# Query features of pairs 16 to 31: transposed by a crossbar DMA of two 16-bit planes instead of on TensorE, in a new order of all work

## The chip, the cores and the metric

One core of one Trainium2 chip. The metric is device time in microseconds, the median of the timed runs; lower is better. The kernel before takes 957.84 us, the median of 3 runs (957.36 to 957.84).

## The reference

Linear attention with random features, then a two-layer perceptron on its output. B = H = 8, S = 576, D = 64, m = 128 features; 4608 tokens of 512 columns, 2048 hidden columns; float32.

```python
def phi(x):
    proj = np.einsum('bhsd,md->bhsm', x, omega)
    h = proj - np.sum(x * x, axis=-1, keepdims=True) / 2.0
    h = h - np.max(h, axis=-1, keepdims=True)
    return np.exp(h) / np.sqrt(m)
q_p, k_p = (phi(q_s), phi(k_s))                 # q_s, k_s: q, k scaled by D ** -0.25
kv = np.einsum('bhsm,bhsd->bhmd', k_p, v)
z = np.sum(k_p, axis=2)
num = np.einsum('bhsm,bhmd->bhsd', q_p, kv)
den = np.einsum('bhsm,bhm->bhs', q_p, z)[..., None] + 1e-06
x = (num / den).transpose(0, 2, 1, 3).reshape(B * S, H * D)
h = x @ w_in
out = (h / (1.0 + np.exp(-h))) @ w_out
```

## The kernel before, in words

**Attention.** The 64 heads are worked on as 32 pairs, numbered n; four pairs are the 512 columns of one batch of 576 tokens. The 2 x 576 tokens of a pair are 9 blocks of 128 tokens (the middle one is shared by the two heads). For the keys (k) and the queries (q) of a pair, TensorE projects onto the 128 features (`project`, L460, its products in L477; the shared block in `project_mids`, L495). VectorE takes maxima and makes biases; ScalarE exponentiates into a tile of 128 tokens by 9 x 128 features, `hk` or `hq` (`expo`, L536, four instructions of 128 columns to a group, one for the shared block; for some pairs `expo_all`, L557, 1152 columns in one). GpSimd adds the key features over blocks (`sums`, L565 to L570), ScalarE rounds the sums (`sums_high`, L574), TensorE adds them over partitions with a matrix of ones (`zsum`, L587), VectorE forms the denominators from `hq` and that (`denom`, L619) and their reciprocals, and GpSimd divides the query features by them (`normal`, L630, three blocks in each of three instructions).

The numerator needs the query features with the feature on the partition. `turn` (L632 to L637) transposes the nine blocks on TensorE, three to a PSUM bank, and `en_copy` (L640) has ScalarE copy each bank into the tile `en`. `kv` (L595) multiplies keys by values; the result is copied (`kt_copy`, L600), transposed (L603) and copied again (`kw_copy`, L608); `numer` (L657) multiplies `kw` by `en`. For later pairs one unit, `kv_numer` (L665), issues the kv of pair n+1 and then the numerator of pair n. ScalarE copies the attention's output out of PSUM (`x_high`, L679).

**Perceptron.** Each float32 operand is held as a high and a low part, and a product is three TensorE passes (`thrice`, L831, 512 columns each; "main products" below). Batches 0 to 2 go through both layers plainly; the other batches are taken in pairs of batches, (1, 2) to (7, 8), as "levels", with sums and differences of quarters multiplied in seven products (`deep`, L895, for the first layer, `product`, L929, for the second). A level's operands are made from the columns of its two batches (`operand_high`, L889, on ScalarE), its results copied or passed through silu by ScalarE (`deep_copy`, L916; `deep_silu`, L919) and stored. Exponentials and silu use different tables of ScalarE, so that each change between them is an ACT_TABLE_LOAD. Weights come by DMA as `w`, from DRAM copies made earlier (`w_d`, `ws_d`).

**Order.** Each step is a unit with an engine (`Plan.add`, L147, with a duration that the planner assumes). The order of all units on all engines is one table of numbers, `RANK`: units are issued in the order of their ranks, so that each engine works through its own in that order and waits for whatever its next one needs. `HOMES` gives the PSUM pool of each product. `RINGS` gives the number of buffers for each name of a tile: before, two of `hq` and two of `en`. All DMAs are issued on one queue, SP's.

Of the kernel before, what the change touches and what calls it, by code (L numbers as in the profile page):

```python
# [9 lines left out]
F32R = mybir.dt.float32r  # L10
U32 = mybir.dt.uint32
# [7 lines left out]
P = 128  # L19
B, H, S, D = 8, 8, 576, 64  # L20
M = 128
# [19 lines left out]
NORM_DVE = tuple(range(9, 12))  # L41
SQUARES = {}
# [27 lines left out]
    "in": 4, "v": 2, "sq": 2, "hk": 2, "hq": 2,  # L70
    "mxk": 2, "mxq": 2, "nbk": 2, "nbq": 2, "mxm": 2, "nbm": 2, "t": 1, "es": 1, "kt": 1, "kw": 2,
    "en": 2, "den": 2, "rd": 2, "g0": 4, "g1": 4, "g2": 4, "g3": 4, "ts": 3, "w": 7, "ic": 2, "c": 3,
# [67 lines left out]
class Plan:  # L140
# [215 lines left out]
)  # L356
HOMES = (
    "aachcahchaccahahcacachaccaacahaahchccchhcccaaccahhcccaahccachccccachhaachahaaaahahaahaaaahaaaahahaah"
    "aahaacachccaccaccacccahcacacccaaccacacccachccaccaccaacachccachacccaaaccaachacahcaaahahahaahahcccahaa"
    "hchacahhahhcaahccchcaahhahahhacahaahchhacchccaahchhaahhhchahahhaaaahhaahaahhahhhhhchaahcahacachhaaah"  # L360
    "ahcachccahchaahhchhchaaahhhahchaachchcaacahhahhachaahcahcaahahchcachaachahhhaacchhahchaaahhhaaa"
)
# [3 lines left out]
def attention_mlp(ctx: ExitStack, tc: tile.TileContext, qX, kX, qS, kS, qT, kT, qn, kn, v, om_in, w_in, w_out, out):  # L366
# [50 lines left out]
    T = {}  # L417
# [1129 lines left out]
```

## Time and profile before

| | before |
|---|---|
| timed runs | 957.84 us, the median of 3 (957.36 to 957.84) |
| profiled execution, its span | 954.4 us |
| TensorE (PE) busy | 942.7 us, 5740 instructions |
| VectorE (DVE) busy | 772.1 us |
| ScalarE (ACT) busy | 619.8 us, 1184 instructions |
| GpSimd (POOL) busy | 392.4 us |
| DMA | 237.87 MB in 103219 packets |

The profiled execution is one run under the profiler; its span runs from the first to the last instruction and is the time against which its rows add up. The timed runs carry what lies around a span too. Busy is time in which an engine had an instruction at work; it is an average over the whole kernel, which has a stage with attention and perceptron together (to about 700 us) and one with the perceptron alone.

### The profile page before, as it was taken

To read this page: it belongs to the slowest core of one execution; us is meant where nothing else is said; L and a number is where in the kernel's file an instruction comes from. 1 tells how busy PE (TensorE), PEld (TensorE's weight loads), DVE (VectorE), ACT (ScalarE), POOL (GpSimd) and SP (SyncE) were. 2 spreads that over 40 slices of the span, in tenths; PEclk is the share of its full clock that TensorE was granted. 3 is DMA by queue.
4 is the path that set the end of the run, shared out by engine and by line. 5 is a ranking of instruction groups with operands and counts; after the bars stand their busy time and mean duration, and the time that the engine had idled before them with its cause. 6 is when DMAs were issued, how large, how long until landed. Compare 5 with 4: busy or idle time off the path is not lost.

```text
span 954.4 us, 16604 instructions
## 1 busy us (share of the span) xinstructions
PE 942.7 (99%) x5740; PEld 771.3 (81%) x5740; DVE 772.1 (81%) x1625; ACT 619.8 (65%) x1184; POOL 392.4 (41%) x430
## 2 busy tenths in 40 slices
PE   9999999999999999999999999999999999999998
PEld 8778888887888888777878888788888878888886
DVE  6899998698648988868988998879999774478964
ACT  7899886788787676897648866663547444225542
POOL 4676567786867676667323234222221000000000
PEclk9999999999999999999999999999999999999999
DMA  6379999989999798957758477646855566556662
GB/s 242 105 222 335 342 343 316 335 320 317 314 327 340 270 353 317 315 192 271 276 165 317 148 270 253 201 166 190 268 187 166 197 246 235 195 188 220 197 212 99
DMA packets 103219, 237.87 MB, mean 249 GB/s; under 512 B 13665, under 2 KB 44513, under 8 KB 103137
## 3 DMA queue, kind: packets, MB, share of 16 engines
q1 hardware_dynamic: 103136, 236.82, 73.0%
q8 instruction: 46, 0.75, 0.3%
q14 instruction: 37, 0.30, 0.1%
HBM read 192.74 MB, written 44.04 MB: 248 GB/s over the span
## 4 chain that ended last, share of the span: by engine, by line
PE 87%; DVE 6%; ACT 3%; DMA 2%; issue 1%; DVEq 0%; ACTq 0%; SPq 0%
PE ps_acc L831 58%; PE ps_h L831 11%; PE ps_att L477 2%; PE ps_att L595 2%; PE ps_h L477 1%; PE ps_att L657 1%; PE ps_h L636 1%; DVE prod L619 1%; PE ps_h L657 1%; PE ps_acc L477 1%; DMA in<-kX 1%; PE ps_h L595 1%; PE ps_acc L636 1%; PE ps_att L636 1%; DMA g<-w_in 1%
## 5 line engine op out<-in xcount | busy, mean ns | idle before, releaser
L831 PE MATMUL ps_acc<-ts,w 128*128 128x512 f32 x2544 | 600.7, 392 | 1.0 <-ACT hk L536 0.5
L831 PEld LDWEIGHTS ps_acc<-ts,w 128*128 128x128 f32 x2544 | 472.0, 188 | 99.0 <-ACT hk L536 0.7
L873 ACT CAST ts<-g 128x1024 fp32r<-128x1024 f32 x112 | 118.3, 1060 | 95.5 <-PE ps_acc L831 86.8
L877 DVE TENSOR_TENSOR ts<-g,ts 128x1024 fp32r<-128x1024 f32 x112 | 144.7, 1300 | 42.7 <-ACT ts L873 42.4
L831 PE MATMUL ps_h<-xq,w 128*128 128x512 f32 x576 | 142.2, 394 | 0.4 <-DVE xq L683 0.4
L831 PEld LDWEIGHTS ps_h<-xq,w 128*128 128x128 f32 x576 | 106.0, 188 | 22.1 <-DVE xq L683 0.9
L923 DVE TENSOR_TENSOR g<-ps_acc,g 128x512 f32<-128x512 f32 x144 | 93.5, 683 | 27.1 <-PE ps_acc L831 26.1
L630 POOL TENSOR_TENSOR hq<-hq,rd 128x384 f32<-128x384 f32 x87 | 81.8, 961 | 80.8 <-DVE rd L625 80.4
L565 POOL TENSOR_TENSOR t<-hk 128x256 f32<-128x256 f32 x64 | 54.8, 869 | 73.6 <-ACT hk L536 45.1
L869 DVE TENSOR_TENSOR g<-g,g 128x1024 f32<-128x1024 f32 x64 | 82.7, 1317 | 0.8 <-ACT g L927 0.6
L578 POOL TENSOR_TENSOR es<-t,es 128x256 fp32r<-128x256 f32 x32 | 27.7, 864 | 85.1 <-ACT es L574 74.0
L745 POOL TENSOR_TENSOR w<-g,w 128x512 fp32r<-128x512 f32 x32 | 46.7, 1474 | 30.7 <-ACT w L741 30.6
L889 ACT CAST ts<-xq 128x1024 fp32r<-128x1024 f32 x21 | 22.3, 1063 | 52.0 <-PE ps_acc L831 46.7
L619 DVE CUSTOM_DVE_ANT_0 prod<-hq,ps_att 128x128 f32<-128x128 f32 (+1 forms) x150 | 42.9, 286 | 10.4 <-PE ps_att L587 5.3
L927 ACT ACTIVATE g<-g 128x1024 f32<-128x1024 f32 x36 | 36.5, 1054 | 13.5 <-DVE g L923 13.4
L446 DVE TENSOR_REDUCE sq<-in 128x9 f32<-128x576 f32 x48 | 34.8, 739 | 11.1 <-ACT in L441 11.1
L570 POOL TENSOR_TENSOR t<-t,hk 64x128 f32<-64x128 f32 x64 | 35.9, 560 | 14.5 <-ACT hk L536 10.7
L950 DVE TENSOR_TENSOR c<-ps_acc,c 128x512 f32<-128x512 f32 x48 | 31.5, 682 | 10.4 <-PE ps_acc L831 10.4
L477 PE MATMUL ps_att<-oms,in 64*128 64x128 f32 x320 | 37.0, 279 | 0.2 <-ACT hk L536 0.2
L893 DVE TENSOR_TENSOR ts<-xq,ts 128x1024 fp32r<-128x1024 f32 x21 | 25.7, 1227 | 12.2 <-ACT ts L889 12.2
L477 PEld LDWEIGHTS ps_att<-oms,in 64*128 64x128 f32 x320 | 32.4, 187 | 3.7 <-issue 1.8
L619 DVE CUSTOM_DVE_ANT_0 prod<-hq,ps_acc 128x128 f32<-128x128 f32 (+1 forms) x100 | 28.6, 286 | 8.4 <-PE ps_acc L587 3.3
(212 smaller groups left out, 1548.3 us busy)
## 6 DMA issues: line engine op xcount, KB each, us to landing
w<-w_d SPq DMA_DIRECT2D x168, 512.0 KB, 4.8
w<-ws_d SPq DMA_DIRECT2D x48, 512.0 KB, 4.6
v<-v SPq DMA_DIRECT2D x32, 320.0 KB, 4.8
out<-c SPq DMA_DIRECT2D x17, 512.0 KB, 4.7
in<-kT SPq DMA_DIRECT2D x24, 352.0 KB, 4.6
in<-qT SPq DMA_DIRECT2D x24, 352.0 KB, 6.2
g<-w_in SPq DMA_DIRECT2D x16, 512.0 KB, 6.2
g<-w_out SPq DMA_DIRECT2D x16, 512.0 KB, 5.8
```

The lines of the kernel that those rows point to most:

```text
L477: nc.tensor.matmul(ps[:, cols], T["raw", n, who][r, o : o + P], oms[r], start=True, stop=True)
L565: nc.gpsimd.tensor_tensor(t[:, i], e[:, 5 * i : 5 * i + 2], e[:, 5 * i + 2 : 5 * i + 4], ALU.add)
L570: nc.gpsimd.tensor_tensor(t[r, i - 3, 0], t[r, i - 3, 0], e[r, MID], ALU.add)
L619: nc.vector.tensor_tensor_reduce(out=prod[r], in0=e[r, c], in1=z[r, j * M : (j + 1) * M], scale=1.0, scalar=GUARD, op0=ALU.mult, op1=ALU.a ...
L630: nc.gpsimd.tensor_tensor(e[:, c], e[:, c], rd[:, c].unsqueeze(2).broadcast_to([P, 3, M]), ALU.mult)
L745: nc.gpsimd.tensor_tensor(lo, T["w", i], hi.bitcast(F32), ALU.subtract)
L831: nc.tensor.matmul(ps, w(a), x[:, b], start=first and n == 0, stop=last and n == 2, **more)
L869: nc.vector.tensor_tensor(out, a, b, ALU.subtract)
L873: nc.scalar.copy(g[:, 0], T["g", p, SOURCE[j], u])
L877: nc.vector.tensor_tensor(g[:, 1], T["g", p, SOURCE[j], u], g[:, 0].bitcast(F32), ALU.subtract)
L923: nc.vector.tensor_tensor(to, T["q", p, chain, i], T["g", p, r, i // 2][:, i % 2], ALU.add)
L927: nc.scalar.activation(g, g, AF.Silu)
```

## The change

For pairs 16 to 31 (`CROSS`) the three `turn` units and three `en_copy` units of a pair are not made. In their place come: `planes` on ScalarE, which copies the normalised query features (as 16-bit words, 2304 to a partition) so that the 1152 first halves of the float32 words stand together and then the 1152 second halves; `cross`, a DMA on SP's queue (`dma_start_transpose`) that transposes the 18 blocks of 128 x 128 16-bit elements from one on-chip tile to another; and `words` on ScalarE, which copies the transposed halves back together into float32. The numerator waits for `words`. Query features, planes, transposed planes and the transposed features share one ring of four buffers, `f`, in place of `hq` and `en` (two each). `RANK` and `HOMES` are new throughout: 3678 units where 3726 were. In the new file the lines behind `normal` stand about 16 further down: `planes` L637, the crossbar DMA L641, `words` L646, `numer` L673, `thrice` L847.

```diff
+CROSS = tuple(range(16, 32))
...
 RINGS = {
...
-    "in": 4, "v": 2, "sq": 2, "hk": 2, "hq": 2,
+    "in": 4, "v": 2, "sq": 2, "hk": 2, "f": 4,
...
-    "en": 2, "den": 2, "rd": 2, "g0": 4, "g1": 4, "g2": 4, "g3": 4, "ts": 3, "w": 7, "ic": 2, "c": 3,
+    "den": 2, "rd": 2, "g0": 4, "g1": 4, "g2": 4, "g3": 4, "ts": 3, "w": 7, "ic": 2, "c": 3,
...
 RANK = (
-    0, 1, 11, 18, 2, 12, 16, 19, 17, 21, 20, 3, 14, 27, 39, 28, 29, 45, 22, 24, 23, 36, 33, 49, 6, 25, 26, 50, 51, 52,
...
+    2, 0, 1, 11, 3, 6, 7, 12, 8, 16, 13, 4, 10, 17, 30, 21, 18, 31, 19, 34, 14, 46, 49, 56, 38, 35, 36, 44, 45, 54, 55,
...
+    def flat(x):
+        return x.rearrange("p c m -> p (c m)")
+
+    def planes(n):
+        T["pl", n] = to = flat(new("f", [P, NC, M])).bitcast(U16)
+        halves = flat(T["h", n, "q"]).bitcast(U16)
+        nc.scalar.copy(to.rearrange("p (b n) -> p b n", b=2), halves.rearrange("p (n b) -> p b n", b=2))
+
+    def cross(n):
+        T["tp", n] = to = flat(new("f", [P, NC, M])).bitcast(U16)
+        nc.sync.dma_start_transpose(out=to.rearrange("p (c t) -> p c t", t=P), in_=T.pop(("pl", n)))
+
+    def words(n):
+        T["en", n] = en = flat(new("f", [P, NC, P]))
+        halves = T.pop(("tp", n)).rearrange("p (b n) -> p b n", b=2)
+        nc.scalar.copy(en.bitcast(U16).rearrange("p (n b) -> p b n", b=2), halves)
...
+            if n in CROSS:
+                continue
             add(("turn", n, g), "PE", 0.246, at(n, 9.5 + 0.1 * g, 44.2 + 0.8 * g), lambda ps, n=n, g=g: turn(n, g, ps),
...
+        if n in CROSS:
+            add(("pl", n), "ACT", 2.1, 0, lambda n=n: planes(n), after=[("norm", n, 2)], alloc=[("f", ("pl", n))], free=[("h", n, "q")])
+            add(("xp", n), "SP", 0.5, 0, lambda n=n: cross(n), after=[("pl", n)], alloc=[("f", ("tp", n))], free=[("pl", n)], lat=4.0)
+            add(("rc", n), "ACT", 2.1, 0, lambda n=n: words(n), after=[("xp", n)], alloc=[("f", ("en", n))], free=[("tp", n)])
```

**TensorE around pairs 18 and 19.** Before, from the products ahead of the transpose of pair 18's kv (L603) on to the kv of pair 20, which is issued with the numerator of pair 19 (`ps_h`, `ps_acc` and `ps_att` are PSUM banks, `ident` the identity for transposes, `ts` and `w` the operands of a main product):

```order
L831 MATMUL ps_acc<-ts,w 128x512 x6
L603 MATMUL ps_h<-ident,kt 128x128
L831 MATMUL ps_acc<-ts,w 128x512 x6
L595 MATMUL ps_h<-hk,v 64x128 x10
L657 MATMUL ps_acc<-en,kw 64x512 x2
L657 MATMUL ps_h<-en,kw 64x64 x2
L636 MATMUL ps_h<-ident,hq 128x128 x3
L636 MATMUL ps_att<-ident,hq 128x128 x3
L603 MATMUL ps_att<-ident,kt 128x128
L636 MATMUL ps_h<-ident,hq 128x128 x3
L587 MATMUL ps_h<-es,ones 128x256 x2
L595 MATMUL ps_acc<-hk,v 64x128 x10
```

and after the change, around the transpose of pair 19's kv (L602) and the kv of pair 20 with the numerator of pair 19:

```order
L847 MATMUL ps_acc<-ts,w 128x512 x6
L602 MATMUL ps_acc<-ident,kt 128x128
L586 MATMUL ps_h<-es,ones 128x256 x2
L594 MATMUL ps_att<-hk,v 64x128 x10
L673 MATMUL ps_acc<-f,kw 64x512 x2
L673 MATMUL ps_att<-f,kw 64x64 x2
L847 MATMUL ps_acc<-ts,w 128x512 x6
L494 MATMUL ps_h<-oms,in 128x128 x2
L847 MATMUL ps_acc<-ts,w 128x512 x36
```

The L636 rows, three transposes each, are gone between the kv and numerator products (L595 and L657 before, L594 and L673 now), and the next 36 passes of main products follow the kv and numerator that are shown, with only a pair of shared-block projections ahead of them.

**ScalarE in that place after the change**, from pair 18's planes copy (its first row) on; the copy at L646 is pair 18's words copy:

```order
L637 COPY f<-f 128x2304
L932 COPY g_5122<-ps_acc 128x512 x2
L535 ACTIVATE hk<-ps_att,nbk 128x128 x4
L935 ACT_TABLE_LOAD
L935 ACTIVATE g_5001<-ps_acc 128x512
L935 ACTIVATE g_5146<-ps_acc 128x512
L607 COPY kw<-ps_att 128x128
L935 ACTIVATE g_5146<-ps_acc 128x512
L646 COPY f<-f 128x2x1152
L535 ACT_TABLE_LOAD
L535 ACTIVATE hk<-ps_h,nbk 128x128 x4
```

and right behind it, from pair 19's planes copy to its words copy and the copy of its transposed kv (the last row), for which the numerator with the main products behind it waits:

```order
L637 COPY f<-f 128x2304
L695 COPY xr<-ps_acc 128x64
L905 CAST ts<-xq 128x1024
L535 ACTIVATE f<-ps_acc,nbm 128x128
L535 ACTIVATE hk<-ps_acc,nbm 128x128
L440 ACTIVATE in<-in 128x576
L599 COPY kt<-ps_acc 128x128
L535 ACTIVATE f<-ps_h,nbq 128x128 x4
L573 CAST es<-t 128x256
L535 ACTIVATE f<-ps_acc,nbq 128x128 x4
L646 COPY f<-f 128x2x1152
L607 COPY kw<-ps_acc 128x128
```

Where before the three copies of a pair (L640) stood close to its numerator, now a copy of 2304 16-bit elements stands before other work of ScalarE and another behind it, with a change of table between them for pair 18.

## Rows read from the trace of the kernel before

**Rows 1.** The page: span, and busy time, share and instructions of each engine.

```profile
span 954.4 us, 16604 instructions
...
PE 942.7 (99%) x5740; PEld 771.3 (81%) x5740; DVE 772.1 (81%) x1625; ACT 619.8 (65%) x1184; POOL 392.4 (41%) x430
```

**Rows 2.** Windows of 100 us: PE, PEld, DVE, ACT, POOL busy (count); clock, DMA share, GB/s.

```profile
400.00:500.00 100.00, 98.43 (x678) 78.11 (x674) 82.76 (x239) 70.30 (x173) 51.59 (x63) 1.00 0.66 229
500.00:600.00 100.00, 100.00 (x606) 81.84 (x606) 91.46 (x182) 74.11 (x147) 33.67 (x33) 1.00 0.71 249
600.00:700.00 100.00, 100.00 (x641) 81.50 (x638) 86.30 (x213) 52.03 (x94) 26.73 (x38) 1.00 0.60 194
```

**Rows 3.** Windows of 20 us, same columns.

```profile
400.00:420.00 20.00, 20.00 (x132) 16.14 (x128) 13.83 (x55) 17.80 (x39) 14.89 (x19) 1.00 0.46 153
420.00:440.00 20.00, 18.52 (x150) 14.10 (x149) 14.02 (x42) 19.35 (x52) 12.27 (x16) 1.00 0.75 258
```

**Rows 4.** TensorE's timeline, 425 to 445 us: start, length, operation [idle before].

```profile
425.43 0.37 PE L477 MATMUL ps_att<-oms,in 64*128 64x128 f32 x1
...
426.52 3.02 PE L831 MATMUL ps_acc<-ts,w 128*128 128x512 f32 x12
429.38 0.49 PE L636 MATMUL ps_acc<-ident,hq 128*128 128x128 f32 x3
429.71 0.49 PE L636 MATMUL ps_h<-ident,hq 128*128 128x128 f32 x3
430.04 0.61 PE L495 MATMUL ps_acc<-oms,in 128*128 128x128 f32 x4
...
432.69 0.50 PE L587 MATMUL ps_att<-es,ones 128*128 128x256 f32 x2 [0.95 <-ACT hk L536]
433.72 1.69 PE L831 MATMUL ps_acc<-ts,w 128*128 128x512 f32 x6 [0.53 <-ACT hk L536]
...
436.84 1.31 PE L595 MATMUL ps_h<-hk,v 128*64 128x128 f32 x20
...
439.06 0.55 PE L636 MATMUL ps_h<-ident,hq 128*128 128x128 f32 x3
```

**Rows 5.** The chain of waits, its longest piece: start, length, engine, tile, line.

```profile
771.68 156.62 PE ps_acc L831 x690
```

**Rows 6.** Groups of TensorE's instructions by shape, line 636: count, busy, mean ns, idle.

```profile
L636 PE MATMUL ps_h<-ident,hq 128*128 128x128 f32 x105 | 17.1, 277 | 0.2
```

**Rows 7.** ScalarE's timeline, 395 to 444 us.

```profile
427.05 0.60 ACT L919 ACTIVATE g<-ps_acc 128x512 f32<-128x512 f32 x1
427.54 1.04 ACT L889 CAST ts<-xq 128x1024 fp32r<-128x1024 f32 x1
428.48 0.60 ACT L919 ACTIVATE g<-ps_acc 128x512 f32<-128x512 f32 x1
...
430.20 1.28 ACT L536 ACT_TABLE_LOAD   x1
431.49 1.14 ACT L536 ACTIVATE hk<-ps_att,nbk 128x128 f32<-128x128 f32 x4
432.51 1.16 ACT L536 ACTIVATE hk<-ps_acc,nbk 128x128 f32<-128x128 f32 x4
433.51 0.42 ACT L536 ACTIVATE hk<-ps_acc,nbm 128x128 f32<-128x128 f32 x1
433.76 0.33 ACT L600 COPY kt<-ps_h 128x128 f32<-128x128 f32 x1
...
435.00 0.80 ACT L441 ACTIVATE in<-in 128x576 f32<-128x576 f32 x1
435.58 0.37 ACT L608 COPY kw<-ps_h 128x128 f32<-128x128 f32 x1
...
439.64 0.48 ACT L640 COPY en<-ps_h 128x384 f32<-128x384 f32 x1
440.02 0.49 ACT L640 COPY en<-ps_att 128x384 f32<-128x384 f32 x1
```

**Rows 8.** Groups of ScalarE's instructions by shape, line 557.

```profile
L557 ACT ACTIVATE hk<-hk 128x1152 f32<-128x1152 f32 x13 | 15.2, 1166 | 2.4 <-DVE hk L546 2.0 <-DVE hk L544 0.3
```

**Rows 9.** Groups of GpSimd's instructions by shape, lines 565, 570, 795.

```profile
L565 POOL TENSOR_TENSOR t<-hk 128x256 f32<-128x256 f32 x64 | 54.8, 869 | 73.6 <-ACT hk L536 45.1 <-ACT hk L557 27.9 <-ACT kt L600 0.4
L570 POOL TENSOR_TENSOR t<-t,hk 64x128 f32<-64x128 f32 x64 | 35.9, 560 | 14.5 <-ACT hk L536 10.7
...
L795 POOL TENSOR_TENSOR ic<-ic 128x256 f32<-128x256 f32 x32 | 28.0, 875 | 2.4
```

**Rows 10.** DMA issues, 380 to 440 us: count, KB each, median us to landing.

```profile
w<-w_d SPq DMA_DIRECT2D x5, 512.0 KB, 6.7
w<-ws_d SPq DMA_DIRECT2D x5, 512.0 KB, 8.2
...
in<-kT SPq DMA_DIRECT2D x4, 352.0 KB, 4.2
```

**Rows 11.** DMA over the whole span: packets and bytes; one kind of issue.

```profile
DMA packets 103219, 237.87 MB, mean 249 GB/s; under 512 B 13665, under 2 KB 44513, under 8 KB 103137
...
out<-c SPq DMA_DIRECT2D x2, 256.0 KB, 2.0
```

More of the change, by code (lines that the diff above doesn't have):

```diff
@@ L10 @@
 F32R = mybir.dt.float32r
+U16 = mybir.dt.uint16
 U32 = mybir.dt.uint32
@@ L168 @@
 RANK = (
[187 rows of a table removed]
[184 rows of a table added]
 )
 HOMES = (
[L358 to L361, printed above, removed]
+    "achaahaccchachcaccahccchaahahccchaccachchahcchcacacchcahccchacccahccccacahaaaaaahaahhaaaaahaahaaahah"
+    "hahahccacahcacccahacaaahcahchcccaacccccaachcaccccacaachccachcahcccacaccchchcahacaahahhaahahahchcahhc"
+    "achahhahacahcacahhacahhahahhahacahahcchachcchcahahahchahcahhahahchaaahchahahcahahhcahchcaachchaacchc"
+    "aahcachccahahaahahahaaahahhhaaacahhaahhcchhahhh"
 )
@@ L479, in project @@
         if n in FOLD or who == "k":
-            T["h", n, who] = new(f"h{who}", [P, NC, M])
+            T["h", n, who] = new("hk" if who == "k" else "f", [P, NC, M])
         if n not in FOLD:
@@ L497, in project_mids @@
         T["pm", n] = ps
-        T["h", n, "q"] = new("hq", [P, NC, M])
+        T["h", n, "q"] = new("f", [P, NC, M])
         T["mxm", n] = new("mxm", [P, 2])
@@ L630, in normal @@
         nc.gpsimd.tensor_tensor(e[:, c], e[:, c], rd[:, c].unsqueeze(2).broadcast_to([P, 3, M]), ALU.mult)
+    def flat(x):
[11 more added lines that the diff above has]
+        nc.scalar.copy(en.bitcast(U16).rearrange("p (n b) -> p b n", b=2), halves)
     def turn(n, g, ps):
         if g == 0:
-            T["en", n] = new("en", [P, NC * P])
+            T["en", n] = flat(new("f", [P, NC, P]))
         for i in range(3):
@@ L1020, in attention_mlp @@
                     order=([("proj", n - 1, "k" if n - 1 in BOTH else who)] if n else []) + ([("mids", n)] if i and not fold else []),
-                    alloc=([(f"h{who}", ("h",) + w)] if fold or not i else []) + ([] if fold else [(f"mx{who}", ("mx",) + w)])
+                    alloc=([("f" if i else "hk", ("h",) + w)] if fold or not i else []) + ([] if fold else [(f"mx{who}", ("mx",) + w)])
                     + [(f"nb{who}", ("nb",) + w)], free=[])
@@ L1037, in attention_mlp @@
                 after=[("raw", n, "k"), ("raw", n, "q"), "omega2"], order=[("proj", n, "k")],
-                alloc=[("hq", ("h", n, "q")), ("mxm", ("mxm", n)), ("nbm", ("nbm", n))], free=[])
+                alloc=[("f", ("h", n, "q")), ("mxm", ("mxm", n)), ("nbm", ("nbm", n))], free=[])
             add(("topm", n), "DVE", 0.34, at(n, 3.5, 6.2 + 5.8), lambda n=n: top_mids(n), after=[("mids", n)])
@@ L1111, in attention_mlp @@
                     after=[("den", n, 2)], order=[("norm", n, g - 1)] if g else [], free=[("rd", n)], port=True)
+            if n in CROSS:
+                continue
             add(("turn", n, g), "PE", 0.246, at(n, 9.5 + 0.1 * g, 44.2 + 0.8 * g), lambda ps, n=n, g=g: turn(n, g, ps),
                 after=[("norm", n, 0 if one else g)], order=[("turn", n, g - 1)] if g else ([("turn", n - 1, 2)] if n else []),
-                alloc=[] if g else [("en", ("en", n))], banks=1, free=[("h", n, "q")])
+                alloc=[] if g else [("f", ("en", n))], banks=1, free=[("h", n, "q")])
             add(("en", n, g), "ACT", 0.37, at(n, 9.6 + 0.1 * g, 44.4 + 0.8 * g), lambda n=n, g=g: en_copy(n, g),
                 after=[("turn", n, g)], free=[bk(("turn", n, g))])
+        if n in CROSS:
+            add(("pl", n), "ACT", 2.1, 0, lambda n=n: planes(n), after=[("norm", n, 2)], alloc=[("f", ("pl", n))], free=[("h", n, "q")])
+            add(("xp", n), "SP", 0.5, 0, lambda n=n: cross(n), after=[("pl", n)], alloc=[("f", ("tp", n))], free=[("pl", n)], lat=4.0)
+            add(("rc", n), "ACT", 2.1, 0, lambda n=n: words(n), after=[("xp", n)], alloc=[("f", ("en", n))], free=[("tp", n)])
         t, k = divmod(n, NPAIR)
@@ L1120, in attention_mlp @@
         x_new = [("xq", ("x", t, k))] if t < ONCE else [] if k % 2 else [("xq", ("xb", t, k // 2))]
-        after = [("kw", n)] + [("en", n, g) for g in range(3)]
+        after = [("kw", n)] + ([("rc", n)] if n in CROSS else [("en", n, g) for g in range(3)])
         free = [("en", n), ("kw", n)]
```

369 rows, old and new, of the table RANK are left out of this document.

## The prediction

> **What bounds the kernel now.** Read the engines' busy shares first: TensorE works in 942.7 of 954.4 us [rows 1], and in the stage the change touches ScalarE has room: 70 of 100 us busy from 400 on, 52 from 600 on, beside 98.4 and 100 on TensorE [rows 2]. So time that TensorE no longer needs is worth its full length, as long as no other engine becomes late. Then ask where another engine is nearly late. In the forty microseconds from 400 to 440, where pairs 17 to 20 come close together because level 1 of the MLP waits for their columns, ScalarE is busy for 17.80 and 19.35 of 20 us, and in the second stretch TensorE falls to 18.52 [rows 3]. The timeline shows why: TensorE stands still 0.95 and 0.53 us until exponentials have run on ScalarE [rows 4]. There ScalarE is the bound already. The change gives work to it.
>
> The profiled execution spans 954.4 us [rows 1]; the median of the timed runs is 957.84, 3.4 more. I work out a difference on the profiled execution and put it on the median.
>
> **TensorE gives up 144 transposes.** Sixteen pairs with nine each. Six in a row start at 429.38, 429.71 and the next operation at 430.04: 0.66 us, 0.11 each [rows 4]; the mean of 277 ns in a group [rows 6] is latency that overlaps. 144 x 0.11 = 15.8 us. Returning to another kind of product costs 0.1 (twelve main products take 2.86 us from 426.52 to 429.38 [rows 4], where the longest unbroken piece of the chain has 690 in 156.62, 0.227 each [rows 5], so 2.72), but most transposes stand beside other small products whose switch stays: 0.7 us in all. **-16.5 us.** All of it is on the path, since TensorE is the bound outside the stretch above. The 1.5 us of standing still in that stretch belong to the old order and go: **-1.5 us.**
>
> **ScalarE gives up 48 copies and gets 32.** A copy of three transposes takes 0.38 us from start to start (439.64 to 440.02 [rows 7]): 48 x 0.38 = 18 us. A planes or words copy has 2304 elements per partition. The nearest row has 1152 in 1.17 us and 0.1 of that overlaps with the next [rows 8]: 2 x 1.07 = 2.1 us. No row has 16-bit operands or a stride of two; the price could be half (1.05, if two narrow elements go in one step) or double. I take 2.1, the nearest row's rate. 32 x 2.1 = 67 us, a net 49 us more. Over the 360 us from 400 on, of which ScalarE has a quarter to a half free [rows 2], this is hidden, except where none is free.
>
> **The stretch of pairs 17 to 19.** I count, in the new order, ScalarE's instructions from the silu that follows level 1's third product of its second operand to the copy of pair 19's kv that pair 19's last product waits for (its end is shown ahead of this). Eight groups of four exponentials at 1.02 (431.49, 432.51, 433.51): 8.2; four single ones at 0.25: 1.0; five table loads at 1.29: 6.5; ten silus and copies of 512 columns at 0.49: 4.9; one cast of 1024: 0.94; two squares at 0.58: 1.2; eight small copies of 0.1 to 0.3, 1.5 in all [rows 7]. That is 24.2, and five planes and words copies make 10.5: 34.7 us, in one queue that cannot be reordered. TensorE's work between the same two points: 54 main products at 0.227, four projections at 1.09 (425.43 to 426.52), two of kv with numerator at 2.22 (436.84 to 439.06), and 2 us of small ones [rows 4, 5]: 23.1 us. The first point needs a product to have finished and the last holds a product up, so TensorE stands still for the difference, **+11.6 us**. What no longer fits is not work in sum but work in this place.
>
> In the same queue stands a wait. The copy of the sums for pair 20 comes 1.8 us of ScalarE's work after the exponentials it depends on; between them GpSimd has five additions at 0.87 and 0.56 [rows 9], 3.7 us, and two of another kind at 0.87 among them. Not waited: 1.9; all waited: 3.6. I take **+2.5 us**.
>
> **The crossbar DMA.** 576 KB from on-chip memory to on-chip memory, 16 of them. No row shows one. Copies of 256 KB land after 2.0 us at best [rows 11]; in 380 to 440, beside the other loads, 352 KB after 4.2 and 512 KB after 6.7 or 8.2 [rows 10]. I take 6.5, just under the shorter of the two rows of the nearest size in this place; ends 2.0 and 8.2. Between a planes copy and its words copy ScalarE has about 5 us of other work for pairs 16 to 18 (for pair 18, in the order shown: two copies, four exponentials, a table load, three silus, a small copy: 4.9). So each of these three is 1.5 us late: **+4.5 us**; pair 19 has 4.6 and the wait above, and is on time. On SP the weight loads, inputs and the v of later pairs queue behind each of these DMAs while it waits for its planes; they are issued some 9 us of products ahead of use, and four to six buffers cover that. I cost them at nothing; if a crossbar DMA holds the queue for its whole landing they lose 4 us of this, and start to be late.
>
> **Pair 23.** The words copy stands behind a copy of a level 1 result (0.5 us), which needs the product just ahead of pair 23's last one; only four projections (0.36 us) lie between on TensorE. 0.5 + 2.1 - 0.4 = **+2.2 us**. The other pairs have 14 to 62 us of TensorE's work between their denominators and their last product and lie within half a microsecond of fitting; I give them nothing at 6.5.
>
> The crossbar's 16 x 0.59 = 9.4 MB beside 237.9 [rows 11] are hidden. Sum: -16.5 - 1.5 + 11.6 + 2.5 + 4.5 + 2.2 = +2.8 us, so **960.6 us**. (0.2%, 1.9 us, is about what a measurement of this kernel can tell.)
>
> **Rivals.**
>
> *Cheap halves.* ScalarE moves 16-bit elements at half price, or DMAs land within the 5 us of cover. With 1.05 per copy the stretch has 29.4 us against 23.1, +6.3 for +11.6, and pair 23 +1.1; with early landings the +4.5 goes. For it: 5 us is well inside the rows; against: nothing here shows a faster copy. The first makes the sum -3.6, the second -1.7, both -8: 954, 956 or 950 us. It decides once the four positive terms make less than 18 us.
>
> *A slow crossbar.* If it lands after 12 us (half more than the longest row), pairs 16 to 19 pay 7 each, 28 for 4.5, and the pairs behind them, with tight fits, a few more: 984 to 995. In its favour: elements of two bytes, and a queue that is busy at 0.75 in this stretch [rows 3]. At 8.2 it is 966, and with planes copies of 4.2 us the stretch alone has 10 more, 971.
>
> *Block by block.* If each of the 18 blocks of 128 by 128 is handled on its own at 1 us (half of the best landing), one takes 18 us and each pair loses 13 beyond its cover; 16 x 13, less some 40 of slack in the roomy pairs: +170, about 1,130. The Trainium skill (VectorE: DVE Perf Modes, The three transpose paths) gives 1309 ns for one such block by DMA and 390 by TensorE. Its TensorE figure is not what this trace shows (0.11 us from start to start), so its DMA figure need not be a rate either; were it one, an estimate from it is 23.6 us per pair and +260 in all.
>
> **How the numbers follow.** The sum with its bounds (957 to 968): 0.50. Cheap halves or early landing: 0.30. Crossbar slow, 968 to 1,000: 0.16. Block by block: 0.04. The range of 8 in 10 reaches from 946 to 985. Faster by over 0.2%: the second case and a little of the first, 0.32. Within 0.2%: 0.19. Slower: 0.49.
>
> **What would show it.** TensorE should have no L636 row for late pairs, and a standstill of 10 us and more between 400 and 440, ended by ScalarE: by words copies ahead of the products of pairs 18 and 19, and by exponentials. ScalarE should be at 20 of 20 there. Planes copies near 2.2 us, crossbar landings 5 to 8. If ScalarE has gaps that end on the crossbar's landing in most pairs, the slow crossbar holds. If TensorE is full from 400 to 440, the count of the stretch is wrong, and the kernel is faster by the 16 us of transposes.

## The result and the profile after

The changed kernel takes 969.8 us (median of 4 runs, 968.99 to 975.07) where the kernel before takes 957.84: ratio 1.0144, 95% interval 1.0117 to 1.0171. The forecast was 960.6 in a range of 946 to 985, on the slower side. The profiled execution spans 968.7 us, 14.3 more than before.

The page's busy times first (they answer [rows 1]). TensorE has 144 instructions and 1.5 us of busy time less, yet its idle time has grown from 11.7 to 27.5 us:

```profile
span 968.7 us, 16331 instructions
...
PE 941.2 (97%) x5596; PEld 759.3 (78%) x5596; DVE 757.5 (78%) x1625; ACT 672.8 (69%) x1168; POOL 385.7 (40%) x430
```

The windows of the changed kernel, in the columns of [rows 2, 3]. ScalarE is busy for 19 to 20 of every 20 us from 400 to 460, TensorE falls to 16.81 and 14.84, and the granted clock falls too, to a mean of 0.83 from 440 to 460 (the third column from the right). The first line is the kernel before in that same window, which is not among the rows ahead (19.91, and a clock of 1.00):

```profile
440.00:460.00 20.00, 19.91 (x135) 15.54 (x134) 18.02 (x44) 12.88 (x37) 15.33 (x17) 1.00 0.90 319
...
400.00:500.00 100.00, 90.61 (x574) 69.86 (x573) 75.02 (x206) 85.70 (x165) 47.86 (x61) 0.97 0.82 257
500.00:600.00 100.00, 98.99 (x600) 78.23 (x599) 94.34 (x201) 82.72 (x146) 28.18 (x31) 1.00 0.73 244
600.00:700.00 100.00, 96.08 (x567) 77.05 (x567) 79.78 (x181) 62.70 (x86) 30.48 (x38) 0.98 0.81 247
...
400.00:420.00 20.00, 19.16 (x126) 15.05 (x125) 15.70 (x51) 19.19 (x37) 13.73 (x17) 1.00 0.70 213
420.00:440.00 20.00, 16.81 (x120) 12.97 (x120) 10.99 (x46) 19.90 (x42) 8.62 (x12) 1.00 0.86 276
440.00:460.00 20.00, 14.84 (x111) 10.56 (x107) 12.42 (x37) 19.06 (x36) 10.31 (x14) 0.83 0.59 181
```

ScalarE's timeline of the changed kernel (against [rows 7]): a planes copy is an L637 row, a words copy an L646 row. From 413.8 to 455 there is no idle time ahead of any row; the first is at 456.33, behind the copy of pair 19's kv (454.80) that TensorE waits for.

```profile
418.13 0.65 ACT L935 ACTIVATE g<-ps_acc 128x512 f32<-128x512 f32 x1
418.80 1.28 ACT L535 ACT_TABLE_LOAD   x1
...
421.57 2.86 ACT L646 COPY f<-f 128x2304 uint16<-128x2304 uint16 x1
...
433.25 2.21 ACT L637 COPY f<-f 128x2304 uint16<-128x2304 uint16 x1
...
440.40 2.81 ACT L646 COPY f<-f 128x2304 uint16<-128x2304 uint16 x1
443.23 1.28 ACT L535 ACT_TABLE_LOAD   x1
444.52 1.14 ACT L535 ACTIVATE hk<-ps_h,nbk 128x128 f32<-128x128 f32 x4
445.54 2.13 ACT L637 COPY f<-f 128x2304 uint16<-128x2304 uint16 x1
...
452.15 2.88 ACT L646 COPY f<-f 128x2304 uint16<-128x2304 uint16 x1
454.80 0.36 ACT L607 COPY kw<-ps_acc 128x128 f32<-128x128 f32 x1
454.95 0.70 ACT L695 COPY xq<-ps_att 128x512 f32<-128x512 f32 x1
456.33 0.58 ACT L695 COPY xq<-ps_acc 128x512 f32<-128x512 f32 x1 [0.69 <-PE ps_acc L673]
```

TensorE's timeline beside it (against [rows 4]), four of the rows that waited, with the length of the wait and what ended it in brackets: a words copy, exponentials, and the kv copy.

```profile
443.26 1.08 PE L673 MATMUL ps_att<-f,kw 128*64 128x512 f32 x4 [1.34 <-ACT f L646]
...
445.72 0.58 PE L476 MATMUL ps_h<-oms,in 64*128 64x128 f32 x1 [1.26 <-ACT hk L535]
...
449.30 3.23 PE L847 MATMUL ps_acc<-ts,w 128*128 128x512 f32 x6 [1.51 <-ACT hk L535]
...
455.21 1.08 PE L673 MATMUL ps_acc<-f,kw 128*64 128x512 f32 x4 [1.05 <-ACT kw L607]
```

The new copies in the groups by shape (count, busy us, mean ns, idle before), which had no row before:

```profile
L646 ACT COPY f<-f 128x2304 uint16<-128x2304 uint16 x16 | 45.2, 2824 | 4.5 <-DMA f<-f 4.4
L637 ACT COPY f<-f 128x2304 uint16<-128x2304 uint16 x16 | 34.2, 2137 | 3.7 <-POOL f L629 2.9 <-DMA f<-f 0.8
```

And the new DMA in the view of DMA issues, with its count and the median us to landing:

```profile
f<-f SPq DMA_TRANSPOSE x16, 3.9
```

A second place stands out, at pair 25: SP is held 5.71 us by the issue of that pair's crossbar DMA (some 2 us for most others), the DMA lands 9.2 us after the start of its issue, ScalarE waits 2.70 us for it and TensorE 2.93 for ScalarE. It is no accident of one execution: in each of the seven further traces with a crossbar DMA for pair 25, it lands after 7.4 to 8.6 us. The three fences are the timelines of SP, ScalarE and TensorE:

```profile
602.63 5.71 SPq L641 DMA_TRANSPOSE f<-f  x1
608.39 1.05 SPq L843 DMA_DIRECT2D w<-w_d  x2
```

```profile
611.95 2.75 ACT L646 COPY f<-f 128x2304 uint16<-128x2304 uint16 x1 [2.70 <-DMA f<-f]
```

```profile
614.75 1.08 PE L673 MATMUL ps_acc<-f,kw 128*64 128x512 f32 x4 [2.93 <-ACT f L646]
```

To put these side by side I priced every one of TensorE's steps (a projection, six main products, a kv with numerator, ...) at the median time, in the trace of before, from its start to the start of the next, for the same kind of step with the same kind behind it. The sum is TensorE's work; what a step took beyond its price is time lost, by standing or at the lower clock. In us, by the changed kernel's times (the columns from "plain DMA" on are experiments below, in their order plain_dma, whole_words_plain, no_copies_plain, splice, late):

| | before | changed | plain DMA | half copies | no copies | splice | late |
|---|---|---|---|---|---|---|---|
| work | 933.5 | 917.4 | 917.4 | 917.4 | 917.4 | 917.9 | 922.4 |
| lost, 0 to 346 | 7.8 | 13.6 | 14.3 | 18.2 | 14.7 | 7.3 | 7.7 |
| 346 to 404 | 0.8 | 1.4 | 1.6 | 1.6 | 1.1 | 0.9 | 0.7 |
| pairs 17 to 21, 404 to 474 | 3.0 | 15.4 | 15.2 | 9.3 | 9.1 | 15.8 | 3.5 |
| 474 to 607 | 1.6 | 5.3 | 5.4 | 4.3 | 4.6 | 5.8 | 5.8 |
| pairs 25 and 26, 607 to 633 | 0.5 | 5.9 | 1.7 | 1.2 | 1.2 | 5.2 | 3.2 |
| 633 to the end | 2.4 | 4.7 | 4.6 | 4.0 | 4.3 | 4.8 | 4.6 |

From before to the changed kernel: -16.1 of work and +30.2 lost, +14.1 in all, beside 14.3 between the spans (about 5 us of each span lie ahead of the first step and behind the last, outside the rows). (The 18.2 under "half copies" hold a wait of 2.6 us for VectorE and 6.83 us at the lower clock in the first 25 us of that one execution.)

### The profile page after: what moved, and what is told of

Its sections match the earlier page's. It is cut to its first block, busy times and chain, and to the rows that moved or that the text cites. A ratio compares the mean times of both kernels' runs of the same rounds, so it can differ in the third digit from the quotient of the medians.

```text
span 968.7 us, 16331 instructions
## 1 busy us (share of the span) xinstructions
PE 941.2 (97%) x5596; PEld 759.3 (78%) x5596; DVE 757.5 (78%) x1625; ACT 672.8 (69%) x1168; POOL 385.7 (40%) x430
## 4 chain that ended last, share of the span: by engine, by line
PE 67%; DVE 14%; ACT 14%; DMA 2%; issue 2%; POOL 1%; DVEq 0%; SPq 0%; ACTq 0%; POOLq 0%
PE ps_acc L847 48%; PE ps_h L847 8%; ACT f L646 2%; DVE g L939 2%; DVE prod L618 2%; PE ps_att L476 2%; ACT f L535 1%; ACT hk L535 1%; PE ps_att L594 1%; ACT L535 1%; DMA f<-f 1%; PE ps_acc L476 1%; PE ps_att L673 1%; DVE mxq L507 1%; DVE ts L909 1%
## 5 line engine op out<-in xcount | busy, mean ns | idle before, releaser
L847 PE MATMUL ps_acc<-ts,w 128*128 128x512 f32 x2544 | 605.5, 394 | 5.2 <-ACT hk L535 1.5
L847 PEld LDWEIGHTS ps_acc<-ts,w 128*128 128x128 f32 x2544 | 472.1, 188 | 110.4 <-DVE g L939 4.4
L847 PE MATMUL ps_h<-xq,w 128*128 128x512 f32 x576 | 142.9, 396 | 0.9 <-ACT f L656 0.4
L847 PEld LDWEIGHTS ps_h<-xq,w 128*128 128x128 f32 x576 | 105.5, 188 | 23.5 <-DVE xq L699 0.6
L629 POOL TENSOR_TENSOR f<-f,rd 128x384 f32<-128x384 f32 x87 | 84.5, 992 | 87.4 <-DVE rd L624 69.0
L564 POOL TENSOR_TENSOR t<-hk 128x256 f32<-128x256 f32 x64 | 51.4, 817 | 100.8 <-ACT hk L535 47.9
L577 POOL TENSOR_TENSOR es<-t,es 128x256 fp32r<-128x256 f32 x32 | 25.4, 793 | 65.6 <-ACT es L573 64.8
L646 ACT COPY f<-f 128x2304 uint16<-128x2304 uint16 x16 | 45.2, 2824 | 4.5 <-DMA f<-f 4.4
L618 DVE CUSTOM_DVE_ANT_0 prod<-f,ps_acc 128x128 f32<-128x128 f32 (+1 forms) x120 | 34.3, 286 | 10.6 <-PE ps_acc L586 5.3
L618 DVE CUSTOM_DVE_ANT_0 prod<-f,ps_h 128x128 f32<-128x128 f32 (+1 forms) x120 | 34.3, 286 | 8.1 <-PE ps_h L586 2.6
L637 ACT COPY f<-f 128x2304 uint16<-128x2304 uint16 x16 | 34.2, 2137 | 3.7 <-POOL f L629 2.9
L569 POOL TENSOR_TENSOR t<-t,hk 64x128 f32<-64x128 f32 x64 | 32.2, 503 | 9.9 <-ACT hk L535 6.1
```

Of the source, the lines that this page charges most:

```text
L564: nc.gpsimd.tensor_tensor(t[:, i], e[:, 5 * i : 5 * i + 2], e[:, 5 * i + 2 : 5 * i + 4], ALU.add)
L618: nc.vector.tensor_tensor_reduce(out=prod[r], in0=e[r, c], in1=z[r, j * M : (j + 1) * M], scale=1.0, scalar=GUARD, op0=ALU.mult, op1=ALU.a ...
L629: nc.gpsimd.tensor_tensor(e[:, c], e[:, c], rd[:, c].unsqueeze(2).broadcast_to([P, 3, M]), ALU.mult)
L646: nc.scalar.copy(en.bitcast(U16).rearrange("p (n b) -> p b n", b=2), halves)
L847: nc.tensor.matmul(ps, w(a), x[:, b], start=first and n == 0, stop=last and n == 2, **more)
```

## The experiments

**The crossbar DMA replaced by a plain one.**

```diff
-        nc.sync.dma_start_transpose(out=to.rearrange("p (c t) -> p c t", t=P), in_=T.pop(("pl", n)))
+        nc.sync.dma_start(to, T.pop(("pl", n)))
```

> The crossbar DMA is replaced by a plain DMA of the same 576 KB from the same tile to the same tile, so the query features of pairs 16 to 31 are not transposed and the output is not the reference's. Theory 1: from 400 to 460 us ScalarE is busy all the time and waits for no DMA, so the standstill there stays within 1 us of what it was; only the waits for landings around pair 25 (2.7 us of ScalarE's idle time, 2.9 of TensorE's) can go; 965 to 970 us. Theory 2 (the crossbar is what is slow): 960 us or less.

966.9 us, ratio 1.0105 (1.0089 to 1.0120). The windows of the stretch are as in the changed kernel, ScalarE full and TensorE at 16.80:

```profile
420.00:440.00 20.00, 16.80 (x114) 12.94 (x113) 11.40 (x50) 19.90 (x39) 7.64 (x11) 1.00 0.82 285
440.00:460.00 20.00, 14.10 (x116) 10.31 (x115) 12.13 (x37) 19.25 (x35) 11.30 (x15) 0.91 0.49 174
```

The loss at pairs 25 and 26 goes (5.9 to 1.7). There the plain DMA lands after 6.5 us, the crossbar after 9.2. So the crossbar, as a slower DMA, costs some 3 us of the 12 (the intervals of the two ratios touch; it is the trace that shows the place), all of it there; in the stretch of pairs 17 to 21 it costs nothing. The first theory holds.

**Half the elements.** On top of the plain DMA, both copies move float32 words.

```diff
-        nc.scalar.copy(to.rearrange("p (b n) -> p b n", b=2), halves.rearrange("p (n b) -> p b n", b=2))
+        nc.scalar.copy(to, flat(T["h", n, "q"]))
...
-        nc.scalar.copy(en.bitcast(U16).rearrange("p (n b) -> p b n", b=2), halves)
+        nc.scalar.copy(en, T.pop(("tp", n)))
```

> As plain_dma, and in addition the planes and words copies copy 1152 float32 words instead of 2304 16-bit halves: the same bytes, half the elements; the features are neither split nor transposed and the output is not the reference's. To be held against plain_dma (966.9). ScalarE's price: 1.1 to 1.2 us per copy if it goes by elements, 2.1 and 2.8 if by bytes. Theory 1 (ScalarE's queue): with 1.1 to 1.2, the five copies of the stretch are 7 us shorter and TensorE's standstill from 400 to 460 falls by 6 to 7 us: 958 to 961 us. Theory 2 (ScalarE's queue is not what holds TensorE): 965 to 967 us whatever the copies cost.

959.4 us, ratio 1.0025 (1.0010 to 1.0040), 7.5 less than plain_dma. The same bytes in half the elements take 1.17 to 1.18 us for 2.14 and 2.82, so the price goes by elements and not by bytes. (The strides of two went with the halves. In the words copies they may have a share; the planes copy's 0.93 ns an element beside 1.02 here shows none.) The groups by shape:

```profile
L636 ACT COPY f<-f 128x1152 f32<-128x1152 f32 x16 | 18.9, 1180 | 7.4 <-POOL f L629 6.5 <-DMA f<-f 0.9
L644 ACT COPY f<-f 128x1152 f32<-128x1152 f32 x16 | 18.7, 1168 | 1.5 <-DMA f<-f 1.4
```

Two planes copies 0.96 shorter and three words copies 1.65 shorter are 6.9 us; the loss in the stretch falls from 15.2 to 9.3, by 5.9. The theory of ScalarE's queue holds as far as this step goes: almost every microsecond taken out of that queue is one that TensorE gets.

**No copies at all.**

```diff
-        T["pl", n] = to = flat(new("f", [P, NC, M])).bitcast(U16)
-        halves = flat(T["h", n, "q"]).bitcast(U16)
-        nc.scalar.copy(to.rearrange("p (b n) -> p b n", b=2), halves.rearrange("p (n b) -> p b n", b=2))
+        T["pl", n] = flat(T["h", n, "q"])
...
-        T["en", n] = en = flat(new("f", [P, NC, P]))
-        halves = T.pop(("tp", n)).rearrange("p (b n) -> p b n", b=2)
-        nc.scalar.copy(en.bitcast(U16).rearrange("p (n b) -> p b n", b=2), halves)
+        T["en", n] = T.pop(("tp", n))
```

> As plain_dma, without any planes or words copy: the plain DMA goes from the divided query features straight to the tile that the numerator reads. The features are not transposed and the output is not the reference's. Theory 1 (ScalarE's queue): against plain_dma (966.9 us, TensorE standing 15 us between pair 17's sums and pair 22's projection) the 12.7 us of the five copies go and the standstill there falls to 3 to 5 us, and another 2 us elsewhere; 952 to 957 us. What is then left above the kernel before's standstill, less 16 us of transposes, is the new order's own. Theory 2 (the order of that stretch is slow by itself): the standstill stays above 9 us, where halving the copies had left it, and 958 us or more.

958.8 us, ratio 1.0020 (1.0010 to 1.0029): a miss for the first theory; it is the second's 958 us or more, with more than 9 us lost in the stretch. The copies that the run before had left cost 1.2 us each, and taking these away gave TensorE nothing more (9.3 to 9.1 lost in the stretch). The windows show that ScalarE is no longer the limit, 11.10 of 20, and what is in its place: 3 us of standing and the clock at 0.83.

```profile
420.00:440.00 20.00, 19.53 (x161) 15.24 (x161) 14.28 (x50) 18.21 (x46) 10.77 (x14) 1.00 0.92 319
440.00:460.00 20.00, 17.11 (x93) 12.65 (x90) 16.36 (x40) 11.10 (x31) 11.79 (x15) 0.83 0.51 178
```

TensorE's timeline names the waits (exponentials, the low part of a level's operand on VectorE, and the sums of pair 20), and then the lower clock: the twenty products of a kv took 1.31 us in [rows 4], and take 2.40 here.

```profile
441.56 0.50 PE L843 MATMUL ps_acc<-ts,w 128*128 128x512 f32 x1 [0.73 <-ACT hk L535]
443.46 2.01 PE L843 MATMUL ps_acc<-ts,w 128*128 128x512 f32 x5 [1.41 <-DVE ts L905]
...
446.22 0.58 PE L586 MATMUL ps_h<-es,ones 128*128 128x256 f32 x1 [0.53 <-ACT es L573]
...
447.53 2.40 PE L594 MATMUL ps_att<-hk,v 128*64 128x128 f32 x20
```

So ScalarE's copies are 6 of the 12.4 us that the changed kernel loses more in this stretch. Behind them lies a second limit, 6 us more than before. Of the 9.1 us lost here 3.45 is standing (400 to 460: 0.09, 0.47 and 2.89, where the kernel before stood 1.57), and 6.83 us at the lower of the two levels are worth up to 3.4. None of the waits ends on the DMA. ScalarE itself now waits for VectorE, longest 5.3 us for a level's operand and 3.1 for a bias of the exponentials. That this is the new order of the stretch is argued, not shown: no run takes the new order and the clock apart.

**The words copy in another order of elements.**

```diff
-        halves = T.pop(("tp", n)).rearrange("p (b n) -> p b n", b=2)
-        nc.scalar.copy(en.bitcast(U16).rearrange("p (n b) -> p b n", b=2), halves)
+        halves = T.pop(("tp", n)).rearrange("p (b n) -> p n b", b=2)
+        nc.scalar.copy(en.bitcast(U16).rearrange("p (n b) -> p n b", b=2), halves)
```

> The words copy goes through its elements in the order of the output (the two halves of a word one after the other, written side by side, read 1152 elements apart) instead of first all first halves and then all second halves. If the 0.68 us by which a words copy (2.82) is longer than a planes copy (2.14) comes from the stride of two on the written side, it falls to 2.1 to 2.2; by theory 1 the three words copies of the stretch then give TensorE 2 us back: 966.5 to 968.5 us. If it comes from anything else, 2.8 and 969 to 970 us.

967.8 us, ratio 1.0116 (1.0095 to 1.0137). The copy falls to 2.41, between the two expectations:

```profile
L646 ACT COPY f<-f 128x2304 uint16<-128x2304 uint16 x16 | 38.5, 2407 | 3.8 <-DMA f<-f 3.8
```

Going through the elements in the order of the output is worth 0.41 of the 0.68 us. How much the stride of two on the written side costs by itself stays open, since the reading changed with it (from side by side to 1152 elements apart). Three copies 0.41 shorter are 1.2 us, and the loss in the stretch falls by about 1; the time lies where the first theory had it.

**The copies on VectorE.**

```diff
-        nc.scalar.copy(to.rearrange("p (b n) -> p b n", b=2), halves.rearrange("p (n b) -> p b n", b=2))
+        nc.vector.tensor_copy(to.rearrange("p (b n) -> p b n", b=2), halves.rearrange("p (n b) -> p b n", b=2))
...
-        nc.scalar.copy(en.bitcast(U16).rearrange("p (n b) -> p b n", b=2), halves)
+        nc.vector.tensor_copy(en.bitcast(U16).rearrange("p (n b) -> p b n", b=2), halves)
```

> All planes and words copies run on VectorE instead of ScalarE, nothing else moves. VectorE has 4 to 9 of 20 us free in each window from 400 to 460. Theory 1 (ScalarE's queue): if such a copy takes 2.4 us or less on VectorE, the standstill from 400 to 460 falls to 2 to 4 us and the time to 957 to 961 us; if it takes over 4 us VectorE becomes the late engine and little is won. Theory 2 (the crossbar's landing holds the products): no change, 968 to 971 us.

1007.2 us, ratio 1.0525 (1.0485 to 1.0564): a miss, though the copies are cheaper there than the expectation asked:

```profile
L646 DVE COPY f<-f 128x2304 uint16<-128x2304 uint16 x16 | 26.0, 1624 | 1.6 <-DMA f<-f 1.5
L637 DVE COPY f<-f 128x2304 uint16<-128x2304 uint16 x16 | 24.7, 1541 | 3.1 <-POOL f L629 3.1
```

The places in the queue had been chosen for ScalarE. VectorE was already busy for 94 of 100 us from 500 to 600 in the changed kernel. Over the whole span TensorE now waits longest for VectorE's words copies (14.4 us in the view of waits). From 400 to 460 ScalarE is no longer full (14.27, 16.03 and 10.98 of 20), and yet TensorE stands 10.4 us there, where it stood 9.2 in the changed kernel: ScalarE's exponentials now wait for their biases, which VectorE makes (10.0 us of such waits). The load has moved to another queue that has no room either, and the run decides nothing between the two theories.

**The new order with TensorE's transposes.** Two kernels put the nine transposes and three copies of a pair where its planes copy stood, for all sixteen pairs and for pairs 16 to 19.

```diff
-CROSS = tuple(range(16, 32))
+CROSS = ()
...
```

(for the second kernel pairs 20 to 31; RANK and HOMES, cut here, are changed to match)

> The new order kept, but all sixteen pairs are transposed by TensorE and copied by ScalarE again, each pair's nine transposes and three copies standing where its planes copy stood. Theory 1 (the new order has ScalarE at its limit from 414 to 455 us only because of the planes and words copies): TensorE has 16 us more work, but the 11 us of standstill between 400 and 460 and the 6 us around 610 to 640 go; what is left is the 6 us that the new order loses in its first 300 us, where nothing was crossed. 965 to 971 us. Theory 2 (the new order as a whole is slower, whoever transposes): the standstill from 400 to 460 stays and the time is 980 us or more. Theory 3 (the order costs nothing, all of the loss is the crossbar and its copies): 957 to 960 us.

> Only pairs 16 to 19 go back to TensorE's transposes, in the place where their planes copies stood; pairs 20 to 31 stay on the crossbar. Theory 1 (ScalarE's queue in that stretch): 36 transposes add 4.1 us to TensorE; the standstill from 400 to 460 us falls from 13 us to about 3; 962 to 965 us, and ScalarE has idle time in the stretch. Theory 2 (the order of that stretch is slow by itself): no less than 969 us, with TensorE still held by exponentials there.

1000.9 and 976.0 us, ratios 1.0466 (1.0446 to 1.0486) and 1.0206 (1.0180 to 1.0232). By their numbers both fall to the second theory (980 or more, no less than 969). But they do not test the order alone. In the place that I gave the transposes one bank serves one group of three after the other, so that a group waits for ScalarE's copy of the one before (13.2 us of such waits in the first kernel, 5.2 in the second), as in this row of the second kernel:

```profile
453.30 0.66 PE L653 MATMUL ps_att<-ident,f 128*128 128x128 f32 x3 [2.23 <-ACT f L657]
```

A further kernel has the transposes of pairs 16, 18 and 19 where their words copies stood, and in different banks.

> Pairs 16 to 19 on TensorE's transposes once more, but the transposes of pairs 16, 18 and 19 stand where the words copies stood (in the first try TensorE reached them before GpSimd's divisions, and transposed through one bank after the other). Theory 1 (ScalarE's queue): 4.1 us more of TensorE's work, 13 us less ScalarE copies in the stretch; standstill from 400 to 460 us down from 13 us to 3 to 6; 963 to 968 us. Theory 2 (the order of that stretch is slow without the copies too): 972 us or more, with ScalarE idle for over 5 of 20 us in the stretch.

969.1 us, ratio 1.0121 (1.0092 to 1.0151; 964.9 to 970.9). The loss in the stretch is 12.1 us, with ScalarE at 13.34 of 20 from 440 to 460 and the clock at 0.83. The time is between the two theories and decides nothing alone. With the run without copies it shows two ways of emptying ScalarE's queue in this order that both lose far more in the stretch than the 3.0 us of the old one.

**The old order up to pair 16.** RANK and HOMES are put together from the old order up to the first maximum of pair 16 and the new one for the rest; at that point four units are done in the one that are not yet done in the other.

> The order of the kernel before up to the first maximum of pair 16 (some 370 us), then the new order for all that is left; the change itself (crossbar, copies, shared ring of four) stays. Theory 1 (the first 300 us lose 6 us to the new order alone): 963 to 965 us, the windows from 100 to 300 us back at TensorE's 99 of 100. Theory 2 (the shared ring, or anything but the order, holds those pairs up): 968 to 970 us.

964.3 us, ratio 1.0076 (1.0058 to 1.0095), as the first theory had it. TensorE's windows in the first stage are those of before again. The first three lines are the splice (the first of them reads 95.15 before and 94.86 in the changed kernel), the next two the kernel before, the last two the changed kernel:

```profile
0.00:100.00 100.00, 95.26 (x810) 80.57 (x811) 85.38 (x243) 88.27 (x198) 62.97 (x77) 1.00 0.71 231
100.00:200.00 100.00, 100.00 (x603) 82.31 (x602) 85.43 (x182) 77.56 (x142) 71.92 (x74) 1.00 0.98 340
200.00:300.00 100.00, 98.97 (x658) 80.30 (x657) 73.22 (x197) 82.39 (x166) 73.35 (x79) 1.00 0.91 314
...
100.00:200.00 100.00, 99.89 (x600) 82.02 (x599) 85.14 (x182) 76.93 (x142) 71.92 (x74) 1.00 0.98 337
200.00:300.00 100.00, 99.04 (x658) 80.30 (x657) 73.48 (x194) 82.73 (x165) 72.01 (x79) 1.00 0.93 318
...
100.00:200.00 100.00, 98.25 (x579) 79.64 (x578) 76.89 (x180) 73.76 (x138) 66.01 (x71) 1.00 0.96 334
200.00:300.00 100.00, 98.25 (x658) 78.66 (x657) 71.44 (x197) 87.65 (x168) 68.29 (x77) 1.00 0.89 313
```

5.5 of the 12 us are thus the new order of work up to pair 16, whose transposes the change does not touch (in the table 6.3 us less are lost up to 346 us).

**Crossing late only.** The old order up to 25 us past pair 19's last product with its transposes, the crossbar for pairs 20 to 31, words copies in the order of the output; and the same with pair 25's kv and numerator behind the projection of pair 27.

```diff
-CROSS = tuple(range(16, 32))
+CROSS = (20, 21, 22, 23, 24, 25, 26, 27, 28, 29, 30, 31)
```

> Only pairs 20 to 31 on the crossbar; the order of the kernel before until about 25 us past pair 19's last product, with TensorE's transposes for pairs 16 to 19 where they stood there, then the new order; words copies in the order of the output. Theory 1 (the loss sits in ScalarE's queue in the stretch of pairs 17 to 19, in the new order's first 300 us, and in the wait around pair 25): twelve pairs spare TensorE 12 us, the stretch and the first 300 us are as before, and of the changed kernel's losses behind 460 us some 9 to 11 stay: 954 to 957 us, level with the kernel before or a little faster. Theory 2 (each crossed pair costs as much as it spares, wherever it stands): 957 to 962 us.

> As late, with pair 25's product of kv and numerator (and the copies of its result and the load of v behind it) moved behind the next main products and the projection of pair 27, 3.6 us of TensorE's work, so that the transposed features have landed when it comes. Theory 1: the wait of 2.9 us around 612 us and the half clock of 3.4 us behind it go: 2 to 4 us less than late, 951 to 954 us. Theory 2 (the wait only moves to the next product that needs ScalarE): the same as late within 1 us.

955.6 us, ratio 0.9994 (0.9980 to 1.0009), and 955.6 us, ratio 0.9984 (0.9973 to 0.9995): the first as its first theory had it, the second as its second had it. The stretch and the first 300 us are those of before (the windows from 400 on read 20.00 and 18.52 as in [rows 3]):

```profile
400.00:420.00 20.00, 20.00 (x130) 16.09 (x125) 14.87 (x56) 18.85 (x43) 14.79 (x19) 1.00 0.46 160
420.00:440.00 20.00, 18.52 (x151) 14.12 (x149) 13.81 (x42) 19.39 (x53) 12.30 (x16) 1.00 0.75 267
```

Of 11.1 us that twelve pairs spare, 9.3 are lost again behind 461 us, and 0.9 more lie behind TensorE's last product. Moving pair 25 takes 1.5 us of loss away in the trace, and nothing from the time (955.56 for 955.60). The expected 2 to 4 us were not there to be won: in the trace of the first kernel TensorE waits 1.73 us at pair 25 and not 2.9, and no lower clock follows. The first cannot be told from the kernel before; the second lies 0.16% under it, hardly more than can be told apart. Both beat the changed kernel.

## Why the prediction was right, and where its sum was not

It forecast slower by 2.8 us and the kernel is 12 us slower, inside the range of 946 to 985. The mechanism, a full queue on ScalarE, and its place were right, though it is only about half of what the stretch loses. The sum gave a cost to two waits that did not come, missed two terms, and mis-sized others. Against the rows it had 4.7 us too much in the stretch and 16.0 too little elsewhere. That the sum fell on the slower side is partly luck: without the 7.0 us for the two waits, of which nothing came, it would have been 4.2 us faster. Of its signs, ScalarE is full and the waits end on a words copy and on exponentials, as it said; but TensorE stands only 4.0 us between 400 and 440, where it gave 10 and more, and 9.2 by 460.

- **-16.5 for the transposes.** TensorE's work is 16.1 us less. Right.
- **-1.5 for the old standstill.** The stretch lost 3.0 before in all, and its waits changed with the order. Not separately visible.
- **+11.6 in the stretch of pairs 17 to 19.** The same two points in the trace of after: the silu at 418.13, then 37.1 us of ScalarE without a gap to 455.2, where 34.7 were counted. Every instruction counted is there. Most of the difference is the three words copies: 8.15 us from start to start for 6.3. The two planes copies (4.02 for 4.2) were priced right. TensorE's count left out the kv of pair 20, 1.14 us, which stands ahead of pair 19's numerator: at the prices of before its steps between the two points come to 24.3 us, not 23.1, and it lost 12.8 there for the 11.6. The count of instructions in one engine's queue between two fixed points was the step that carried the forecast. What it did not say is what lies behind: the run without copies gets only 6 us of it back.
- **+2.5 for the sums of pair 20 and +4.5 for the crossbar in this stretch.** Both came to nothing. ScalarE stands nowhere from 413.8 to 455: it was so late that the sums and the DMA (3.9 us for 6.5) were there before it. The two waits were added to a queue that they are parallel to. The wait for the sums comes out once the copies are gone: ScalarE then stands 2.49 us for them. So the stretch with its waits was forecast at 17.1 more than before and gave 12.4.
- **+2.2 at pair 23.** About 1 us of the 3.7 that are lost more from 474 to 607. **Nothing for the pairs behind it** was wrong by 5.4 us at pairs 25 and 26, where the landing after 9.2 us, not the distance in the order, made the wait. From 600 to 604 us, around that issue, the DMA engines are busy for 0.99 of the time, and the plain DMA lands late in the same place too (6.5); that the other loads are the cause is argued, not shown. Behind 633 us 2.3 us more are lost in small pieces, which no run explains.
- **Nothing for the first 350 us** was the largest term that it missed: 5.8 us. RANK and HOMES are new throughout and so moved the first sixteen pairs too, and the prediction looked at the new order only where the diff's new steps stand.

Of the rivals, the slow crossbar fell: 16 landings at a median of 3.9 us, and a plain DMA in its place lands after 3.5 (4.2 and 6.6 in the two other runs with a plain one). The Trainium skill (Advanced Engine Details and Errata, X-Bar Transpose (TRN2)) has transposing DMAs on this chip as fast as regular ones; this trace agrees to 0.4 us of 3.5 at the median, not at pair 25 (9.2 beside 6.5). Block by block fell too: 18 blocks in 3.9 us are 0.22 us each. The Trainium skill (VectorE: DVE Perf Modes, The three transpose paths) gives 1309 ns for one; as a rate, this trace contradicts it by a factor of six. Cheap halves fell in its first half and came true in its second: 16-bit elements cost ScalarE about as much each as 32-bit ones (0.93 and 1.22 ns beside 1.02), while the DMAs did land within the 5 us of cover, and the +4.5 went, as it said. Its sum of -1.7 did not follow, because the terms that the forecast missed were larger.

## What to carry to other kernels

Before work is taken off the bound engine and given to another, count that other engine's queue between two points where the bound engine hands over and takes back, in the new order and with every copy, table load and copy-back in it: idle time summed over a stage says nothing about the forty microseconds in which both are nearly full. Waits that run beside a full queue are not added to it; they come out when the queue is shortened. And when a change brings a new order of everything, the stages that it doesn't mention have to be read too: here the first 350 us alone, with the old order put back, returned 5.5 of the 12 us.

## What the runs showed of the hardware

- A copy of 2304 16-bit elements on ScalarE takes 2.14 us with a stride of two on the side that is read, 2.82 with it on the side that is written, 2.41 written in order and read 1152 elements apart; 1152 float32 elements take 1.17. On VectorE the first two of these copies take 1.54 and 1.62.
- The 576 KB crossbar transposition lands after 3.9 us at the median and 9.2 us at pair 25; its issue holds SP's queue some 2 us, 5.7 in the worst case, and no weight load is issued meanwhile. The issue of the plain DMA of the same bytes holds it 0.5 us.
- TensorE's granted clock fell from 1.00 to 0.5 (from the higher to the lower of its levels) after TensorE had stood still: in the changed kernel for 6.8 us from 445.6 on, behind waits of 1.29 and 1.34 us and at the end of one of 1.26, and for 3.4 us from 616 on, behind one of 2.9. In the kernel before it never fell before the last microseconds. In the stretch at 446 it cannot have cost the changed kernel much, since ScalarE, which TensorE waited for, had no gap there.
